# A new order of loads and of steps, and tiled matmuls for the first batch, in a kernel of windowed attention followed by two large products

## The chip, the cores and the metric

The kernel runs on one core of a Trainium2 chip. Time is the device time of one execution in microseconds (us), as the median of a kernel's runs. Each execution has a state: slow, when it is over 1.5% longer than the fastest of the same kernel, otherwise fast. The ratios below are the record's: fast runs of one kernel against fast runs of the kernel before in the same rounds on the same chip, with a 95% interval, so they are not quite the ratio of the medians beside them, which are of all runs. Where a ratio is turned into us, it is multiplied by 352, the median of the kernel before.

## The reference

```python
# q, k, v: 8 batches x 8 heads x 576 x 64;  w_in: 512 x 2048;  w_out: 2048 x 512
scores = scale * q @ k.T              # kept where 0 <= row - column < 64
attn   = softmax(scores) @ v
x = attn.transpose(0, 2, 1, 3).reshape(4608, 512)
h = x @ w_in
g = h - tanh(h)
out = g @ w_out
```

The 4608 rows of x are worked in nine chunks of 512. A batch is 576 rows, so a chunk needs one or two batches.

## The kernel before

A chunk takes 16 steps of the first product ("h", four matmuls of 512 columns into one bank of PSUM, the memory that TensorE writes its results to, then a tanh on ScalarE and a subtraction on VectorE that gives the bank back) and 16 steps of the second ("y", also four matmuls; four such steps fill a bank, which ScalarE then copies out). The order of steps alternates: one h of this chunk, one y of the chunk before.

```python
def hp_mm(c, m):                       # one h step
    hp = ps[:, m % 2, :]               # two banks in turn
    for ki in range(4):
        nc.tensor.matmul(hp, w_in_tile(ki, m), chunk_tile(c)[...], start=(ki == 0), stop=(ki == 3))
    th = sm_pool.tile([128, TOK], F32, tag="th", name="th")
    nc.scalar.activation(th, hp, ACT.Tanh)
    return hp, th

def g_sub(c, m, hp, th):
    nc.vector.tensor_tensor(gT[c][:, m, :], hp, th, ALU.subtract)

def yp_bank(c, s):
    return (0, 2)[s % 2] if c == NC - 1 else 2      # one bank for y, except in the last chunk
# ... (cut)
LAG = 16
for h in range(min(items), 2 * (16 * NC + LAG) + 2):
    n = h // 2
    # even h: hp_mm of step n;  odd h: yp_mm of step n - 16
    # then whatever of attention is listed for this step (items), then g_sub
```

Attention and loads are listed per step. The part ahead of the first step, the prologue, is a script. Of its letters, `V1`, `K1`, `Q1` are loads of the second batch, `w0` to `w2` pieces of w_in, `k05s` and the like the copies of V that give the keys of one window (vw from vb, nine to a batch; the last letter is the issuing engine: p GpSimd, s SyncE, a ScalarE; VectorE then copies what they brought from the upper 64 partitions of vw to the lower 64, which is called the shift), `P0` a second product of attention with its normalization:

```python
PLAN = {
    -1: """ ... k08s k00s b1p k03p n k02s F0a E0av R01 R02 q2p E1av k07p V1 k06a a3p k04p b2v K1 a2a
            R00 F1v k05s r3a E2aa F2a Q1 w0 R10 z0v ... P0 R11 E3aa R20 P1 ... w1 ... Q2 R32 P3 ...""",
    # ... (cut)
    12: "a8v R41 o2 o1 a9p d20p z1v",
    15: "R50 o3 R40 ... o0 d23p P5 k25s R60",        # o0 to o3: the pieces of w_out
```

The softmax here doesn't subtract the row's maximum and nothing guards it: scores larger than these inputs give would overflow.

## Time and profile before

| kernel before | |
|---|---|
| time | 351.54 us, median of 3 (351.35 to 354.38) |
| span of the profiled run | 351.4 us |
| TensorE busy (PE) | 315.1 us, 90% |
| VectorE, ScalarE | 199.0 and 192.8 us |
| first matmul of the first product | 38.2 us |
| first product of the second chunk | 70.7 us |

TensorE is the bound once the prologue is over. To read its stretches, compare the length with the busy time of PE. The second and third chunk (columns: stretch, length, busy us of PE, PEld, DVE, ACT, POOL, then clock, DMA share and GB/s; PE is TensorE's matmuls, PEld its weight loads, DVE VectorE, ACT ScalarE, POOL GpSimd, further on SP SyncE, and a q behind a name is that engine's instruction queue):

```profile
71.70:107.00 35.30, 33.72 (x247) 19.02 (x246) 23.91 (x38) 20.49 (x38) 14.61 (x19) 1.00 0.79 148
107.00:142.40 35.40, 35.04 (x263) 20.14 (x261) 24.56 (x40) 22.26 (x42) 17.32 (x22) 1.00 0.78 134
```

A chunk lasts some 35 us and TensorE works in all but 0.4 to 1.6 us of it. VectorE and ScalarE are busy for two thirds of that time, which says nothing about how soon a single bank comes back; this matters below.

### The profile page before, as it was taken

What the parts mean: (1) busy time and instruction counts of PE and PEld (TensorE: products, weight loads), DVE (VectorE), ACT (ScalarE), POOL (GpSimd) and SP (SyncE); (2) the same over time, 40 slices, a digit from 0 to 9 for tenths busy, and PEclk for the clock granted to TensorE, in tenths of its full rate; (3) what the DMA queues carried; (4) which work ended last, traced back from release to release, by engine and by line L of the source; (5) the groups of instructions that cost most, each with busy time, mean ns of one, the idle gap of its engine ahead of it and who ended that gap; (6) DMA issues with size and microseconds to landing.
All of it is one profiled execution on the core that took longest, in us unless ns stands there. A gap on an engine that the chain in (4) does not pass through costs nothing.

```text
span 351.4 us, 5740 instructions
## 1 busy us (share of the span) xinstructions
PE 315.1 (90%) x2173; PEld 179.0 (51%) x2173; DVE 199.0 (57%) x314; ACT 192.8 (55%) x347; POOL 112.0 (32%) x160
## 2 busy tenths in 40 slices
PE   0267788899899999999999999997999999999995
PEld 0256366555555555555555555553555444444442
DVE  1336786867676666666776766663656333344400
ACT  1467479765556665666566666652554444444411
POOL 7829543833338325422642264410000000000000
PEclk9988999999999999999999999998999999999999
DMA  8699999969777696958494895669711400010021
GB/s 175 126 164 190 175 189 173 183 133 180 161 148 112 127 137 146 139 126 156 102 160 105 164 169 123 130 147 206 189 46 38 121 32 30 31 60 30 30 89 62
DMA packets 54436, 43.98 MB, mean 125 GB/s; under 512 B 25144, under 2 KB 48248, under 8 KB 54024
## 3 DMA queue, kind: packets, MB, share of 16 engines
q0 software_dynamic: 20512, 18.22, 35.8%
q1 hardware_dynamic: 33128, 24.37, 27.0%
q10 hardware_dynamic: 768, 1.02, 1.0%
q8 instruction: 17, 0.28, 0.3%
q14 instruction: 11, 0.09, 0.1%
HBM read 36.70 MB, written 11.21 MB: 136 GB/s over the span
## 4 chain that ended last, share of the span: by engine, by line
PE 78%; DVE 7%; DMA 5%; ACT 5%; POOL 2%; issue 2%; SPq 0%; ACTq 0%; DVEq 0%; POOLq 0%
PE ps L324 34%; PE ps L304 32%; PE ps L261 5%; PE ps L247 4%; DVE xs L272 3%; PE ps L234 3%; DMA vw<-vb 3%; DMA vall<-in_v_dram 2%; DVE gT L314 2%; ACT th L308 1%; DVE qt L84 1%; ACT pt L251 1%; ACT qt L82 1%; DMA kt<-kd 1%; DVE pt L255 1%
## 5 line engine op out<-in xcount | busy, mean ns | idle before, releaser
L314 DVE TENSOR_TENSOR gT<-ps,th 128x512 bf16<-128x512 f32 x144 | 99.3, 691 | 94.9 <-ACT th L308 92.6
L304 PE MATMUL ps<-xT,wi 128*128 128x512 bf16 x576 | 147.7, 380 | 1.7 <-DVE gT L314 1.7
L324 PE MATMUL ps<-w_out_sb,gT 128*128 128x512 bf16 x576 | 146.1, 381 | 0.2 <-ACT ysb L329 0.2
L308 ACT ACTIVATE th<-ps 128x512 f32<-128x512 f32 x144 | 85.9, 597 | 79.8 <-PE ps L304 79.5
L304 PEld LDWEIGHTS <-wi 128*128 128x128 bf16 x576 | 61.4, 114 | 47.7 <-issue 3.6
L324 PEld LDWEIGHTS <-gT 128*128 128x128 bf16 x576 | 54.3, 98 | 55.9 <-issue 1.0
L251 ACT ACTIVATE pt<-ps 128x384 bf16<-128x384 f32 x96 | 46.9, 490 | 44.9 <-PE ps L247 38.3
L272 DVE TENSOR_TENSOR xs<-ps,rc 64x576 bf16<-64x576 f32 x64 | 48.3, 755 | 1.5
L84 POOL COPY vb<-vall 72x1024 bf16<-72x1024 bf16 x29 | 30.6, 1069 | 52.8 <-DMA vall<-in_v_dram 40.2
L247 PE MATMUL ps<-qt,kt 128*128 128x128 bf16 x288 | 36.4, 226 | 8.5 <-ACT pt L251 3.8
L261 PEld LDWEIGHTS <-pt 128*128 128x128 bf16 x288 | 22.7, 101 | 19.8 <-issue 3.6
L261 PE MATMUL ps<-vw,pt 128*128 128x130 bf16 x288 | 29.6, 226 | 3.4 <-DVE xs L272 1.1
L247 PEld LDWEIGHTS <-kt 128*128 128x128 bf16 x288 | 24.4, 102 | 12.1 <-DMA kt<-kd 2.1
L329 ACT ACTIVATE ysb<-ps 128x512 f32<-128x512 f32 x36 | 21.5, 597 | 16.0 <-PE ps L324 16.0
L84 DVE COPY qt<-ps 64x576 bf16<-64x576 bf16 x24 | 18.2, 759 | 18.1 <-ACT qt L82 18.1
L84 POOL COPY kb<-kall 96x768 bf16<-96x768 bf16 x26 | 21.7, 837 | 13.0 <-DMA kall<-in_k_dram 12.1
L84 POOL COPY qb<-qall 96x768 bf16<-96x768 bf16 x24 | 20.0, 832 | 16.8 <-DMA qall<-in_q_dram 16.8
L82 ACT ACTIVATE qt<-ps 64x576 bf16<-64x576 bf16 x32 | 20.3, 636 | 1.0 <-PE ps L234 0.6
L82 ACT ACTIVATE kt<-ps 128x576 bf16<-128x576 bf16 x25 | 16.2, 648 | 4.3 <-PE ps L234 4.0
L255 DVE TENSOR_TENSOR pt<-pt,ps 128x1152 bf16<-128x1152 bf16 x24 | 17.9, 745 | 0.0
L234 PE MATMUL ps<-ident,kb 96*128 96x96 bf16 x168 | 12.2, 210 | 2.7 <-ACT xT L82 0.9
L234 PEld LDWEIGHTS <-kb 96*128 96x128 bf16 x168 | 10.2, 100 | 7.4 <-issue 2.7
(52 smaller groups left out, 123.4 us busy)
## 6 DMA issues: line engine op xcount, KB each, us to landing
out_dram<-ysb SPq DMA_DIRECT2D x36, 256.0 KB
vall<-in_v_dram POOLq DMA_DIRECT2D x7, 576.0 KB, 10.0
kall<-in_k_dram POOLq DMA_DIRECT2D x7, 576.0 KB, 8.8
qall<-in_q_dram POOLq DMA_DIRECT2D x7, 576.0 KB, 8.8
vw<-vb SPq DMA_DIRECT2D x61, 65.0 KB
vw<-vw SPq DMA_DIRECT2D x6, 520.0 KB
w_out_sb<-in_moe_w_out_dram POOLq DMA_DIRECT2D x4, 512.0 KB, 8.4
qd<-qz SPq DMA_DIRECT2D x4, 288.0 KB
```

The source lines that it names most:

```text
L82: nc.scalar.activation(o, i, ACT.Copy)
L84: eng.tensor_copy(o, i)
L234: nc.tensor.transpose(tp[:, e, :], src[:, e, :], ident[:P, :P])
L247: nc.tensor.matmul(sp[:, i, :], kT[g % NR][:, 64 * j:64 * j + 128], qT[g % NR][:, :, 64 * j:64 * j + 64], start=True, stop=g >= 2 * NP)
L251: nc.scalar.activation(PT[g % NPT][:, 3 * grp:3 * grp + 3, :], sp, ACT.Exp, scale=scale)
L261: nc.tensor.matmul(ps[:, 5 + grp, 130 * i:130 * i + 130], PT[g % NPT][:, j, :], vw[b % 2][:, j, 2 * pr:2 * pr + 2, :], start=True, stop=True)
L272: nc.vector.tensor_tensor(xo[r, :, :, pr, :], ov[r, :, :, h, 0:D], rc[r].to_broadcast([64, 3, 3, 64]), ALU.mult)
L304: nc.tensor.matmul(hp, w_in_tile(ki, m), chunk_tile(c)[:, :, ki % 2, 64 * (ki // 2):64 * (ki // 2) + 64], start=(ki == 0), stop=(ki == 3))
L308: nc.scalar.activation(th, hp, ACT.Tanh)
L314: nc.vector.tensor_tensor(gT[c][:, m, :], hp, th, ALU.subtract)
L324: nc.tensor.matmul(yp, gT[c][:, m, s * 128:(s + 1) * 128], w_out_sb[:, m, :], start=(m == 0), stop=(m == M - 1))
L329: nc.scalar.activation(ysb, ps[:, yp_bank(c, s), :], ACT.Copy)
```

## The change

It means to shorten the prologue. The first batch's attention uses tiles of 64 rows or columns of the TensorE array, with VectorE's normalization in one instruction over all partitions. Both weights are loaded ahead of the second batch. The first chunk goes through both products alone, so that TensorE has work while the second batch arrives. Cut to its core:

```diff
+    def pair_of(banks):
+        a, b = banks
+        return ps[:, a:b + 1:b - a]
+    def tile_scores(g, grp, banks):   # ... 64-row tiles, one exponential over a pair of banks
+    def tile_pv(g, banks):            # ... 64-column tiles, one normalization over a pair of banks
 def hp_mm(c, m):
-        hp = ps[:, m % 2, :]
+        hp = ps[:, m % 3 if c < 2 else m % 2, :]
 def yp_bank(c, s):
-        return (0, 2)[s % 2] if c == NC - 1 else 2
+        return (2, 0)[s % 2] if c == NC - 1 or (c < 2 and s < 2) else 2
+    HS = [0, 32] + [30 * c for c in range(2, NC)]       # step at which each chunk's h begin
+    MOE = []
+    for c in range(NC):
+        ys = len(MOE) - M * c
+        y_left = M * c - ys
+        end = HS[c + 1] - HS[c] if c + 1 < NC else 2 * M
+        hs = [("h", c, m) for m in range(M)]
+        early = [("y",) + divmod(ys + i, M) for i in range(min(y_left, end - M))]
+        late = [("y",) + divmod(ys + len(early) + i, M) for i in range(end - M - len(early))]
+        # ... 16 h with the early y spread among them
+        MOE += mixed + late
+    # first batch: cast V, warm(9), tile_scores(0, 0, (0, 4)), tile_scores(0, 1, (1, 7)), warm(6),
+    # keys_v(0, ...), load_w_in(0), ... load_w_in(1), ... load_w_out(0..3)
+    for pr in range(NP):
+        at(3, load_v, 1, pr)
+    for g in range(4, 8):
+        at(4, load, g, "k", G)
+        at(4, load, g, "q", G)
+    for j in range(NJ):
+        at(22, keys_v, 1, j, Y if j < 5 else A)
+    # ... second batch's attention at steps 24 to 31, third batch's at 33 to 58
+    for j in range(NJ):
+        at(33 + j // 3, keys_v, 2, j, Y)
-    LAG = 16
-    for h in range(min(items), 2 * (16 * NC + LAG) + 2):   # h and y in alternation
+    for h, op in enumerate(MOE):
```

`warm(n)` issues n matmuls whose result is not used.

## The prediction

> **What bounds the kernel now.** I read the page's slices first, then a table of busy times in stretches, then the chain of work that ended last in order of time, then the timelines of GpSimd (it issues the loads) and of TensorE.
>
> The slices (each 8.8 us):
>
> ```profile
> PE   0267788899899999999999999997999999999995
> ...
> PEclk9988999999999999999999999998999999999999
> DMA  8699999969777696958494895669711400010021
> ```
>
> From the ninth slice TensorE is at 9 in nearly every slice, and the DMA row falls. In the first eight it is the other way round: the DMA is at 9, TensorE is not. The stretches make it exact (columns: stretch, its length, busy us of PE, PEld, DVE, ACT, POOL, then clock, DMA share, GB/s):
>
> ```profile
> 20.00:30.00 10.00, 6.63 (x68) 5.86 (x69) 4.53 (x8) 6.53 (x12) 3.90 (x4) 0.66 1.17 192
> ...
> 50.00:55.00 5.00, 3.42 (x61) 3.09 (x59) 3.91 (x7) 4.27 (x9) 2.72 (x4) 1.00 1.00 145
> ...
> 65.00:70.00 5.00, 4.13 (x29) 2.27 (x28) 3.81 (x8) 3.58 (x8) 4.63 (x7) 1.00 1.01 194
> 70.00:80.00 10.00, 10.00 (x64) 5.21 (x62) 5.87 (x10) 6.38 (x12) 4.36 (x5) 1.00 0.69 127
> 80.00:90.00 10.00, 10.00 (x81) 6.00 (x80) 7.59 (x12) 5.57 (x10) 2.61 (x4) 1.00 1.05 203
> ```
>
> Up to 70 us the DMA share is about 1; from 70 us TensorE is busy 10.00 of 10.00. So there are two stages: a prologue of some 70 us bound by transfers and by short dependent steps, and 280 us bound by TensorE alone. The chain shows what the prologue waits for:
>
> ```profile
> 2.93 6.30 DMA vall<-in_v_dram
> ...
> 16.57 9.21 DMA vw<-vb
> 25.86 0.71 DVE vw L167
> 26.61 0.61 PE ps L261 x4
> ...
> 33.67 0.77 DVE xs L272
> ...
> 40.81 1.04 PE ps L304 x4
> ```
>
> The keys' copy of V (vw from vb), issued at 16.57, lands only after 9.21 us, behind the second batch's V, whose load was issued at 14.96. Then four rounds of product, reciprocal and two half-height multiplications run one after the other, and the first matmul of the first product (L304) starts at 38.2. The GpSimd timeline shows the loads' order:
>
> ```profile
> 33.18 0.80 POOL L176 DMA_DIRECT2D wi<-in_moe_w_in_dram  x1
> ...
> 34.74 0.81 POOL L101 DMA_DIRECT2D qall<-in_q_dram  x1
> ...
> 37.85 0.76 POOL L176 DMA_DIRECT2D wi<-in_moe_w_in_dram  x1
> ...
> 48.74 0.97 POOL L151 DMA_DIRECT2D vall<-in_v_dram  x1
> 51.37 1.12 POOL L184 DMA_DIRECT2D w_out_sb<-in_moe_w_out_dram  x2
> ...
> 62.28 0.53 POOL L184 DMA_DIRECT2D w_out_sb<-in_moe_w_out_dram  x1
> ```
>
> The third batch's Q, K and V stand between the weights. The last piece of w_out took about 7 us and so landed at 69.3; the second product (L324) starts at 71.8, when 17 of the 144 steps of the first have been done in 34 us, for want of anything else to feed TensorE.
>
> **What the Trainium skill says.** "DMA: Bandwidth & Descriptors", Issuing engines are not separate DMA queues: DMAs started by any engine share the same 16 DMA engines and interleave. The trace agrees: the copy above took 9.2 us beside a load, others 3.9 us. So the order of issue decides what arrives first. "TensorE: Matmul & The Clock Gate", Back-to-back issue gap: N/2.4 + 2.5 ns, 216 ns for 512 columns; here four such matmuls take 0.86 us, so agreed. The same page, What's actually happening: the clock is halved when TensorE has idled and comes back after some 3.4 us of work; here 0.66 in 20 to 30 us. The added dummy matmuls aim at that. "TensorEngine Tiling (Array Packing)", PSUM Bottleneck: tiling speeds up TensorE but not the evacuation of PSUM. No run here shows tiles yet. I take it as the reason to count the tiles' gain on VectorE and ScalarE, not on TensorE.
>
> **The change, part by part.**
>
> First batch in tiles. Per head pair the multiplication is one over 128 partitions x 640 in place of two of 64 x 576 (755 ns each, so 1.51 us); by its columns one takes about 0.84 us. The exponentials are two (640 and 512 columns) in place of three of 384 (490 ns). Between 384 columns (490) and 512 (597) a column costs 0.84 ns, so 0.70 + 0.60 = 1.30 us against 1.47. Q is evacuated once on ScalarE (0.65) in place of ScalarE then VectorE (0.64 + 0.76). VectorE so saves about 1.4 us per pair in the round that is the chain: four rounds of some 1.1 us instead of 2.0. Tiled matmuls with 64 or 65 columns I put at the 43 ns of a 96-column transposition: 20 x 43 ns is 0.86 us per pair for the second product of attention, against 0.51 before. That is 0.35 us worse, hidden in the first batch, and 1.4 us in the second.
>
> Keys earlier. The casts of V move to ScalarE and VectorE right after its landing (8 to 9.5 us), so the nine copies are issued at about 11 to 14 us, with no second batch's V ahead of them, and land at 18 to 20 us instead of 25.9. Shift (1.4), four rounds (4.4), transpositions and their evacuation (1.5): the first product starts at about 27 us instead of 38.2.
>
> Weights ahead of the second batch. From the landings between 34.8 us (first w_in piece) and 62.5 (second w_out piece), 8.8 MB of float32 arrived in 27.7 us, 318 GB/s. Over the first 75 us, with copies and gaps, it is 20.2 MB, 278 GB/s. The first batch (3.5 MB) and all weights (8.4 MB) at 278 GB/s from 2.2 us on: 45 us. The first chunk's 16 steps of the first product run from 27 to 41 us, and its second product needs the last w_out piece after three more steps, 44 us: a stall of 1 to 2 us. The order of instructions shows a further tie: a GpSimd load waits for the one eight places earlier, so V of the second batch waits for w_in, and K for w_out; with the others still in flight this should not empty the queues.
>
> First chunk alone, then the second batch. After the first chunk all of its 32 steps are done. The second batch's data are complete at 2.2 + 15.5 MB / 278 GB/s = 58 us. After the last K: cast 0.83, transpositions and evacuation 1.2, then in TensorE's order three and a half steps (3.0), six score groups of 0.33 us (2.0), three tiled products (2.6), transpositions of x (1.0) and about 1 us of VectorE and ScalarE latency at the end: 11.6 us. The second chunk therefore starts at about 69.5 us.
>
> Added at the end of the prologue: x of the third batch is transposed on TensorE, 18 x 56 ns = 1.0 us. Chunks of 30 steps instead of 32 let the first product run ahead; TensorE's sum is unchanged.
>
> Sum. From the second chunk on there remain 256 steps of four matmuls of 512 columns, at 0.8632 us: 221.0. Attention: 20 head pairs with transpositions 0.52, scores 0.50, product 0.51, 30.6 in all; four pairs without transpositions 4.0; x 1.0. Together 256.6. Check on the kernel before: at 71.8 us 271 steps (233.9) and 32.3 us of attention remain, 266.2; its last matmul ends at 347.4, so 9.4 us went to waits (5.2 us named in TensorE's timeline, 1.9 of them for kt from kd at 240 us; the clock of 0.68 after that wait cost some 1.8 more). I keep 9.4, as the later batches' code is the same. From the last matmul to the end 4.0. So 69.5 + 256.6 + 9.4 + 4.0 = 339.5. Against 351.5: TensorE has done 15 more steps (12.9 us) at a time 2.3 us earlier, less about 3.3 us of third-batch attention that is not yet done or is added.
>
> **The rivals.** First: the second batch comes too late, and the wait moves from the weights to it. For it: the ring of eight, the V path (cast 4.2 us on GpSimd, copies, shift) that holds all of the TensorE order behind its first tiled product, and ScalarE's some 14 us of work in that part. Against: DMA is fed continuously. It would put the second chunk at 75 us: 345. Second: a pure stretch of first products needs 0.60 us of ScalarE and 0.69 of VectorE per 0.86 us of TensorE, so once the third batch's attention is mixed into the second chunk, VectorE and ScalarE can bound it. For it: VectorE's sum there is about 15 us against TensorE's 17.6, close with in-order engines. Against: three banks instead of two for the first product. It would cost 2 to 4 us: 342. Third: the new spacing also removes the late wait for kt from kd and its halved clock; that gives 3 to 4 us more: 336. Fourth: transfers alone set the prologue and nothing is gained; against it, 278 GB/s would then have to fall below 230, which only the first 20 us show.
>
> **Range and chances.** The start of the second chunk is uncertain by about 4 us, the waits by 3. I predict 339.0 us, with 333.5 to 345.0 holding it 8 times in 10. Faster by over 2% means below 344.5: 0.87. Within 2%: 0.11. Slower: 0.02.
>
> **What would show it.** In the changed kernel the copies to vw should land by 20 us; the first matmul of the first product should start at 25 to 29 us; the last w_out piece land near 45; the first product of the second chunk start at 67 to 72; TensorE be busy over 95% from there; and its last matmul lie 4 us before the end. The first product starting after 33 us would fell the step on tiles and keys; a gap over 3 us before the second chunk, named by vall, kall or vw, would mean the first rival; gaps named by ScalarE or VectorE in the second chunk, the second.

## The result, and the profile after

The changed kernel takes 397.67 us (median of four runs, 394.19 to 400.45, the slowest of them slow, so that the ratio rests on three) against 351.97 us for the kernel before in the same rounds: ratio 1.1221 (1.113 to 1.1311). It is slower by 43 us, where 12 us less were predicted. The profiled run was fast: span 392.5 us, clock 0.965.

The slices of the changed kernel, each 9.8 us:

```profile
PE   6668996689488878778887899799989999999995
...
PEclk9975999889879999999999999999999999999999
DMA  9999959374605774672776458785696031001012
```

TensorE starts earlier, as was meant. But from the seventh slice to the twenty-third it is mostly at 8 or below, where the kernel before stood at 9 in nearly all from its ninth slice on. The DMA row is no longer full either, so transfers are not what fills these slices. The stretches of the changed kernel's second-batch part and next three chunks:

```profile
51.30:87.30 36.00, 27.04 (x278) 16.93 (x282) 12.24 (x22) 13.31 (x28) 15.63 (x19) 0.91 0.71 122
87.30:135.20 47.90, 37.03 (x277) 21.55 (x282) 26.19 (x41) 25.11 (x48) 12.93 (x17) 0.93 0.49 86
135.20:178.00 42.80, 33.77 (x247) 19.47 (x250) 24.14 (x37) 22.48 (x43) 17.65 (x23) 1.00 0.66 119
178.00:218.00 40.00, 33.73 (x238) 19.05 (x240) 22.96 (x36) 21.51 (x40) 13.23 (x18) 1.00 0.60 106
```

Compare with the two lines of before: TensorE's work is 37.0 us in the second chunk and then 33.8 and 33.7, much as before, and the chunks are 5 to 13 us longer. Some records are missing (542 of 576 second-product matmuls are in the trace; 34 at 0.216 us are 7 us), so the idle time is overstated by up to that in all.

To follow this through all kernels I use one mark, the start of the first tanh of a chunk in the trace, and at the end the last copy of y. In us, with chunk 1 the first:

| kernel (profiled run) | 1 | 2 | 3 | 4 | 5 | 6 | 7 | 8 | 9 | last y |
|---|---|---|---|---|---|---|---|---|---|---|
| before | 39.4 | 71.9 | 108.2 | 143.3 | 178.6 | 212.4 | 249.1 | 279.2 | 306.8 | 347.5 |
| after | 36.8 | 88.2 | 136.2 | 178.8 | 218.9 | 255.6 | 291.2 | 321.2 | 347.1 | 388.6 |

The predicted sum can be set against this, line by line: the second chunk's first matmuls came at 87.3 us (one alone at 86.7) in place of 69.5 (17.8 us). From there to the last matmul, at 388.5, are 301.2 us; 256.6 us of work were counted, so 44.6 us lie beyond it, in place of 9.4 (35.2 us). They are not all waits: the trace has TensorE idle for 35.7 us there (overstated by up to the 7 us above), and the rest is work that took longer than counted, part of it at half clock (0.50 from 105.7 to 112.5 us). In the kernel before, the idle time from 71.8 us on is 5.2 us. The tail is 4.0 us, as predicted. 339.5 + 17.8 + 35.2 = 392.5 us, the span (the run's time, 394.19 us, is 1.7 us longer). So there are two things to explain: a late second chunk, and slow chunks after it.

### The profile page after: what moved, and what is told of

It reads as the page before. It is cut to its first block, busy times and chain, and to the rows that moved or that the text cites. A ratio compares the mean times of both kernels' runs of the same rounds, so it can differ in the third digit from the quotient of the medians.

```text
span 392.5 us, 5974 instructions
## 1 busy us (share of the span) xinstructions
PE 330.6 (84%) x2277; PEld 182.5 (47%) x2312; DVE 196.4 (50%) x316; ACT 186.6 (48%) x339; POOL 111.9 (29%) x159
## 4 chain that ended last, share of the span: by engine, by line
PE 61%; DVE 13%; DMA 13%; ACT 8%; issue 2%; SPq 1%; POOL 0%; ACTq 0%; DVEq 0%; POOLq 0%
PE ps L346 26%; PE ps L366 24%; DVE xs L313 5%; DMA vw<-vb 4%; DMA vw<-vw 4%; DVE gT L356 3%; PE ps L302 3%; DMA xT<-xs 3%; DVE qt L85 2%; PE ps L238 2%; PE ps L288 2%; DMA qall<-in_q_dram 2%; ACT th L350 1%; ACT pt L266 1%; ACT ysb L371 1%
## 5 line engine op out<-in xcount | busy, mean ns | idle before, releaser
L366 PE MATMUL ps<-w_out_sb,gT 128*128 128x512 bf16 x542 | 138.0, 382 | 14.2 <-ACT ysb L371 9.7
L346 PEld LDWEIGHTS <-wi 128*128 128x128 bf16 x576 | 62.3, 114 | 61.3 <-issue 15.4
L292 ACT ACTIVATE pt<-ps 128x384 bf16<-128x384 f32 x84 | 40.7, 488 | 45.5 <-PE ps L288 35.9
L313 DVE TENSOR_TENSOR xs<-ps,rc 64x576 bf16<-64x576 f32 x48 | 36.2, 755 | 1.1
L371 ACT ACTIVATE ysb<-ps 128x512 f32<-128x512 f32 x36 | 21.4, 595 | 27.1 <-PE ps L366 22.8
L85 POOL COPY kb<-kall 96x768 bf16<-96x768 bf16 x29 | 23.9, 827 | 35.2 <-PE ps L238 19.2
L288 PE MATMUL ps<-qt,kt 128*128 128x128 bf16 x252 | 29.7, 223 | 3.2 <-ACT pt L292 2.0
L302 PE MATMUL ps<-vw,pt 128*128 128x130 bf16 x216 | 23.4, 223 | 6.5 <-DMA vw<-vw 6.5
L302 PEld LDWEIGHTS <-pt 128*128 128x128 bf16 x216 | 17.8, 99 | 21.3 <-issue 4.7
L288 PEld LDWEIGHTS <-kt 128*128 128x128 bf16 x252 | 20.9, 100 | 12.3 <-issue 3.8
L85 POOL COPY qb<-qall 96x768 bf16<-96x768 bf16 x20 | 16.6, 828 | 10.4 <-DMA qall<-in_q_dram 6.0
L83 ACT ACTIVATE qt<-ps 64x576 bf16<-64x576 bf16 x24 | 15.3, 636 | 3.2 <-PE ps L238 3.1
```

The lines of the kernel that those rows point to most:

```text
L83: nc.scalar.activation(o, i, ACT.Copy)
L85: eng.tensor_copy(o, i)
L288: nc.tensor.matmul(sp[:, i, :], kT[g % NR][:, 64 * j:64 * j + 128], qT[g % NR][:, :, 64 * j:64 * j + 64], start=True, stop=g >= 2 * NP)
L292: nc.scalar.activation(PT[g % NPT][:, 3 * grp:3 * grp + 3, :], sp, ACT.Exp, scale=scale)
L302: nc.tensor.matmul(ps[:, 5 + grp, 130 * i:130 * i + 130], PT[g % NPT][:, j, :], vw[b % 2][:, j, 2 * pr:2 * pr + 2, :], start=True, stop=True)
L313: nc.vector.tensor_tensor(xo[r, :, :, pr, :], ov[r, :, :, h, 0:D], rc[r].to_broadcast([64, 3, 3, 64]), ALU.mult)
```

## The experiments

Two theories were set against each other. A: the order of steps. An h with no y behind it asks for its bank again too soon, and a run of y in one bank waits for each copy. B: the order of loads and copies. The second and third batch come late, and TensorE, which works in the order of the program, stops at them.

### The order of steps

**Runs in the kernel before.** Only the order of steps is changed there, in chunks three to seven (counted from one, as everywhere below outside the quoted texts; the texts count the first chunk as 0, or not at all): 16 h with 6 y among them, then 10 y.

```diff
+    EARLY = 6
+    for c in range(2, 7):
+        # 16 h, the first EARLY y spread among them, then the other y
+        ORDER[32 * c:32 * c + 32] = mixed + ys[EARLY:]
```

> The kernel before with one thing of the change alone: in chunks 2 to 6 the 32 steps are no longer first product, second product in turn, but 16 first products with 6 second ones among them, then 10 second ones in a run (the changed kernel has 4 to 12 among, then 10 to 2). Loads, tiles and the attention's slots stay. Theory A, the order of the steps costs the time (in a run of first products the tanh and the subtraction do not hide, in a run of second ones the single bank waits for its evacuation): each of the five chunks grows by 3 to 6 us, total 366 to 380. Theory B, the order is harmless and the later chunks are slow because data come late: within 1.5% of before, under 357.

Measured: 381.33 us, ratio 1.0748 (1.071 to 1.0785), output correct. Chunks three to seven take 45, 39, 41, 39 and 35 us where before has 35, 35, 34, 37 and 30. So the order alone costs 26 us in a kernel whose loads, copies and tiles are untouched. That is just above theory A's range, and theory B's "no change" is refuted.

The timeline of TensorE in this run shows one such wait (start, length, what, and in brackets the idle time before it and what ended it):

```profile
196.80 1.03 PE L304 MATMUL ps<-xT,wi 128*128 128x512 bf16 x4
...
197.92 1.03 PE L304 MATMUL ps<-xT,wi 128*128 128x512 bf16 x4
...
200.56 1.02 PE L304 MATMUL ps<-xT,wi 128*128 128x512 bf16 x4 [1.44 <-DVE gT L314]
```

These are three h steps one after the other with two banks. The third needs the first one's bank, which comes back after 200.56 - 196.80 = 3.76 us: four matmuls, the tanh behind whatever ScalarE has in hand, the subtraction behind whatever VectorE has. In the kernel before, the same bank is asked for later:

```profile
144.30 1.03 PE L304 MATMUL ps<-xT,wi 128*128 128x512 bf16 x4
...
148.60 1.03 PE L304 MATMUL ps<-xT,wi 128*128 128x512 bf16 x4
```

Here one h lies between the two (at 146.36), and two y: 4.30 us. The y steps in between are what hides the round trip.

**Twelve among.** The same with 12 of the 16 y among the h, so that 4 h of a chunk and not 10 are bare (have no y behind them).

```diff
-    EARLY = 6
+    EARLY = 12
```

> As the run with runs in the kernel before, but 12 of the 16 second-product steps stand among the 16 first-product steps of chunks two to six, and 4 in a run after them, where that run had 6 and 10. Theory A (the cost is first-product steps with no second-product step behind them): 4 bare steps instead of 10, so 0.4 of its 27 us: 360 to 367 us, chunks two to six at 36 to 38 us. Rival (what costs is the attention standing at other places, whatever the length of the runs): 373 to 385 us.

Measured: 363.39 us, ratio 1.0308 (1.0248 to 1.0369), as theory A expected. The waits of TensorE over the whole run, for the bank of the first product (on gT) and of the second (on ysb), as total us, times, longest. The kernel before (its ysb wait is 0.2 us, in the page's groups):

```profile
PE ps L304 <- DVE gT L314: 1.7, 3, 0.6
```

Twelve among:

```profile
PE ps L304 <- DVE gT L314: 6.1, 13, 0.9
PE ps L324 <- ACT ysb L329: 5.0, 5, 1.1
```

Six among:

```profile
PE ps L304 <- DVE gT L314: 18.6, 23, 1.7
...
PE ps L324 <- ACT ysb L329: 8.8, 10, 1.1
```

In all three kernels 1.7 us of the gT wait fall in the first chunk. With 20 bare h steps in five chunks the two waits are then 9.4 us there, with 50 they are 25.6 us: 0.47 and 0.51 us for each. The times rise by 11 and 26 us, 0.54 and 0.53 us a bare step. (In both traces 31 of the 576 second-product matmuls are missing, so the waits are overstated somewhat.) The dose, the named waits and the total time agree.

**A second bank for y.** In the changed kernel, some runs of y get a second bank.

```diff
     def yp_bank(c, s):
+        if (c, s) in ((2, 0), (3, 0), (4, 0), (5, 0)):
+            return 0
+        if (c, s) == (2, 1):
+            return 1
```

> The changed kernel with the second product's result alternating between two banks where its steps run one after another in chunks 2 to 5. Theory A: the waits of second-product steps for the evacuation (9.7 us in all in the changed kernel) fall to about 4, the time by 4 to 6 us. Rival B: TensorE then waits at the next data instead, time within 1%.

Measured: 397.91 us, ratio 1.1278 (1.1215 to 1.134), so no gain. The wait for ysb, 9.7 us in the changed kernel, is gone from the top of the list, and in its place h waits 6.4 us for the transposed x of the next batch (three times, up to 3.9 us), while the wait for gT stays at 8.4 us. A wait that is taken off a run of y is spent at the next tie. The rival's number is met; that the whole order was late there is argued, not shown. The y half of theory A was not worth mending alone.

**Alternation in the changed kernel.** The changed kernel with the order of before from the second chunk on; attention is moved to the steps that correspond.

```diff
-    HS = [0, 32] + [30 * c for c in range(2, NC)]
+    HS = [0] + [32 * c - 16 for c in range(1, NC)]
+    MOE = [("h", 0, m) for m in range(M)]
+    for c in range(1, NC):
+        for m in range(M):
+            MOE += [("h", c, m), ("y", c - 1, m)]
+    # second batch's attention all at step 15
```

> The changed kernel, its tiles, loads, banks and dummy matmuls kept, but the step order of the kernel before: the first chunk's 16 first-product steps alone, then from the second chunk on one first-product step and one second-product step of the chunk before in turn; the attention's slots are moved with it. The second chunk then starts with none of the first chunk's second product done, so TensorE idles through the second batch: its start at 78 to 86 us. Theory A, the order of steps is what makes the later chunks slow: from there each chunk takes 33.7 to 36 us as in the kernel before, so 256.6 + 13.8 + 9 + 4 after a start near 82: 365, range 358 to 371, though 16 more steps are left at that point than in the changed kernel. Theory B, later data are late: chunks stay at 37 to 48 us, total 385 or more.

Measured: 384.06 us, ratio 1.0877 (1.0826 to 1.0928), but the output was wrong. The second batch's attention at step 15 wrote into bank 0 before the subtraction of that same step, which came after it in the program, had read it. The program's order itself was wrong. The time lies between what A and B expected, and is read no further. Mended, with the subtraction of that step ahead of the attention:

> The changed kernel with the order of steps of the kernel before, as in the alternate run, with its fault mended: the subtraction of the first chunk's last step now stands ahead of the second batch's attention, which wrote over its bank. Theory A (the order of steps): correct output, 380 to 388 us, chunks four and later back at 33 to 36 us each, so some 12 us less than the changed kernel. Rival (the speed came from the wrong output or from the fault): 392 to 400 us.

Measured: 383.24 us, correct, ratio 1.0861 (1.0803 to 1.0918). That is 0.036 below the changed kernel, or 13 us, give or take some 4, as theory A expected; the rival's 392 to 400 is refuted. The profiled run, with a clock of 0.554, is not read; the ratio is of its three fast runs. In the changed kernel the two named waits are

```profile
PE ps L366 <- ACT ysb L371: 9.7, 10, 1.3
PE ps L346 <- DVE gT L356: 8.4, 15, 1.6
```

18.1 us in all, 17.1 of them in chunks three to eight, which have 42 bare steps (0.41 us each). The second chunk, whose h have three banks, has none of the two. So the order, with the slots of attention, casts and loads and the banks of y that moved with it, is worth 13 us of the 43; that other waits take up the rest of the 17 is likely, but not shown, and whether the later chunks went back to 33 to 36 us this run can't say.

### The first batch

**Neighbouring banks.** The scores of one pair of heads use banks (0, 4) and (1, 7). `pair_of` addresses such a pair as one strided slice, and the program's tracking of dependences seems to take all that lies between as touched. The changed kernel's timeline shows what this does to the scores' second group, in banks 1 and 7, which waits for the exponential of banks 0 and 4:

```profile
10.80 0.59 PE L257 MATMUL ps<-hide,ident 128*128 128x256 bf16 x2 [2.02 <-ACT pt L266]
```

```diff
-    tile_scores(0, 0, (0, 4))
-    tile_scores(0, 1, (1, 7))
+    tile_scores(0, 0, (0, 1))
+    tile_scores(0, 1, (4, 5))
     # and so for every pair of banks
```

> The changed kernel with the pairs of PSUM banks that a tile's evacuation reads made neighbours (0 and 1, 4 and 5, 6 and 7) instead of 0 and 4, 1 and 7, 0 and 7. The built program then lacks the waits of the second score group, of the dummy matmuls and of second-product steps for an evacuation of banks that they do not share. Theory C, these waits hold the prologue: the first matmul of the first product at 29 to 31 us instead of 34.6, the second chunk at 78 to 83 instead of 87.3, total 5 to 9 us less. Rival, transfers and casts set the prologue: first product not before 33, total within 1%.

Measured: 389.51 us, ratio 1.102 (1.0993 to 1.1047), 7 us less than the changed kernel. The mark of the first chunk falls from 36.8 to 34.3 us and that of the second from 88.2 to 81.0: most of the gain is in the second batch, whose banks were tied in the same way. The first matmul came at 32.0 us, a little after the 29 to 31 expected; the rival's "not before 33" is refuted. With the ties gone, another wait ends last in the first batch. TensorE has the scores of the first two pairs of heads done at 16.4 us and then waits for the shift (5.43 us until 22.55), and the shift for a copy of V, of which the chain of this run says:

```profile
14.10 9.42 DMA vw<-vb
```

SyncE issued it at 13.09 us, behind the first piece of w_in (12.62).

**No idle matmuls.** `warm(6)` and `warm(2)` are taken out.

```diff
-    warm(6)
-    warm(2)
```

> The changed kernel without the six and two dummy matmuls between the first batch's head pairs (the nine at the start stay). They run at the halved clock (six took 2.72 us) ahead of the second pair's transpositions. If they stand in the way: first product 2 to 3 us earlier, total 2 to 3 us less. If they keep the clock up, more matmuls run at half clock and the first product starts within 1 us of 34.6 or later.

Measured: 396.44 us, ratio 1.1266 (1.1205 to 1.1328), the same as the changed kernel. The first chunk is 1.4 us earlier (35.4), the second no earlier in effect (88.0). The six stood on the chain for 2.72 us at half clock. They did bring the full clock, from 16.9 to 23.8 us, where without them it is 0.50 from 9.4 to 36.7; yet the chunk comes earlier without them, and the gain is lost by the second. Neither expectation fits quite.

**The first batch without tiles.** `scores` and `pv` with `norm` in place of `tile_scores` and `tile_pv`.

```diff
-    tile_scores(0, 0, (0, 4))
-    tile_scores(0, 1, (1, 7))
+    scores(0, 0, 4)
+    scores(0, 1, 0)
+    scores(0, 2, 1)
     # and so for the four pairs of heads; pv and norm in place of tile_pv
```

> The changed kernel with the first batch's attention as in the kernel before (128 x 128 and 128 x 130 matmuls, three exponentials, two half-height multiplications), all else kept. The prediction put the tiles' gain at about 0.9 us per head pair: first product 3 to 5 us later, total 3 to 5 us more. Theory C's rival, that the tiles' bank pairs cost what they save: first product within 1.5 us of 34.6, total within 1%.

Measured: 404.4 us (395.77 to 411.51), ratio 1.1283 (1.1191 to 1.1376), correct. Two of its four runs were slow, so the ratio rests on two. Its profiled run was slow too, so its 40.1 us for the first chunk (3.3 later than with tiles) is only an indication. The ratio's interval covers that of the changed kernel: whatever the tiles give, it does not reach the end clearly.

### Loads and copies

**Keys early.** In the changed kernel the copies that give the second batch its keys are listed at step 22, four of them issued by ScalarE. Its DMA queues, ScalarE's first, then SyncE's:

```profile
55.01 4.79 ACTq L162 DMA_DIRECT2D vw<-vb  x4
```

```profile
56.11 7.81 SPq L162 DMA_DIRECT2D vw<-vb  x5
64.08 23.98 SPq L373 DMA_DIRECT2D out_dram<-ysb  x3
88.24 6.49 SPq L162 DMA_DIRECT2D vw<-vb  x9
```

V of the second batch had been cast by 50.8 us, but step 22 came at 55. The third batch's copies stand behind three outputs in SyncE's queue, which works in order: they go out at 88.24. The experiment lists both earlier, all on SyncE:

```diff
-        at(22, keys_v, 1, j, Y if j < 5 else A)
+        at(16, keys_v, 1, j, Y)
-        at(33 + j // 3, keys_v, 2, j, Y)
+        at(30, keys_v, 2, j, Y)
```

> The changed kernel with the second batch's copies of V for the keys given right after the first chunk's first product and all by SyncE (not by SyncE and ScalarE after six steps of the second product), and the third batch's at slot 30 instead of 33 to 35. Theory D, those copies hold the second chunk: first tiled product of the second batch at 60 to 63 us instead of 69, second chunk at 80 to 83 instead of 87.3, total 4 to 7 us less. Rival: the second batch's ScalarE and VectorE work is the bound there: second chunk within 2 us of 87, total within 1%.

Measured: 387.98 us, ratio 1.0969 (1.0926 to 1.1013), 9 us less than the changed kernel. The second chunk did not come earlier (mark 90.1, against 88.2): the copies went out from 50.5 us on, but the shift that follows them on VectorE still began only at 68.0. It came straight after VectorE's evacuation of the second batch's last transposed q (67.22, 0.76 us): it stands behind two of these in VectorE's order, so the order of steps held it, and not the copies. The second batch's first product came at 69.5 us (69.1 in the changed kernel), so neither that nor the second chunk came as theory D expected, though the total fell by more than it said. The gain is in the chunk after it: third mark 131.0 in place of 136.2, and the third batch's copies went out at 71.4. In the changed kernel TensorE waits there for the third batch's shifted V,

```profile
105.74 1.03 PE L302 MATMUL ps<-vw,pt 128*128 128x130 bf16 x8 [4.60 <-DMA vw<-vw]
```

and its clock is 0.50 from there to 112.5 us. With the keys early both are gone.

**Weights first in the kernel before.** One part of the change alone: all of w_in ahead of the second batch, whose keys are then turned inside the first chunk.

```diff
-   ... E1av k07p V1 k06a a3p k04p b2v K1 a2a
+   ... E1av k07p w0 w1 w2 V1 k06a a3p k04p b2v K1 a2a
     # w0, w1, w2 taken from where they stood
-        0: "b8p",
+        6: "b4v b7v b5p F4a b6p b9p E4vv b8p",     # taken from the script ahead of step 0
```

> The kernel before with only the order of loads of the change: the whole of the first weight ahead of the second batch, and the second batch's keys turned inside the first chunk instead of ahead of it. Theory B (weights first moves the first product little and the second batch's attention late): first product 0 to 4 us earlier than the 39 us of before, second chunk not earlier than 71.9, 349 to 358 us. Rival (the prediction's own reading, that the first product is bound by the loads ahead of it and everything after moves with it): first product 5 us or more earlier and 343 to 347 us.

Measured: 366.27 us, ratio 1.0409 (1.0353 to 1.0465), slower by 14 us; both theories missed. The first chunk's mark is at 49.8 us, ten later than before. The chain of this run, and what GpSimd had issued just ahead of it:

```profile
18.40 17.94 DMA vw<-vb
```

```profile
14.53 2.27 POOL L176 DMA_DIRECT2D wi<-in_moe_w_in_dram  x3
```

The last of the first batch's key copies, 65 KB, is issued behind all of w_in and the second batch's V and takes 17.94 us to land; in the kernel before it took 9.21 us behind that V alone. The changed kernel pays some 3 us of this. It issues its nine copies between 10.2 and 14.5 us, w_in from 12.88 on. The four that GpSimd issued, all ahead of w_in, landed in 3.8 to 4.3 us each; but the last two of SyncE's five went out behind w_in's first piece, and VectorE's second shift waited for a copy until 23.24 us. This run's 14 us are therefore not the changed kernel's loss; it shows which neighbour a small copy must not have.

**Keys first, in the kernel before.** The opposite, as it was meant: the nine copies ahead of the second batch's V. This is the step of the prediction on the keys, tried by itself.

```diff
-   k08s k00s b1p k03p n k02s ... E1av k07p V1 k06a a3p k04p b2v
+   k08s k00s b1p k03p k07p k04p n k02s ... E1av k06s V1 a3p b2v
```

> The kernel before with one part of the change: all nine copies of the first batch's keys are issued ahead of the second batch's V load. If the prologue's chain carries through: first product at 34 to 36 us (39.4 before), 346 to 349 us. Rival (the second chunk waits for the last piece of the second weight, landed at 69.3 us, whatever the first product does): first product earlier as well, second chunk still at 71 to 72 us, 350.5 to 353 us.

Measured: 354.41 us, ratio 1.0051 (0.9999 to 1.0104): the same. The first chunk did not come earlier: mark 39.2 against 39.4. The edit does less than was meant. Seven of the nine copies go out ahead of the second batch's V (issued at 15.14 us), but one, `k05s`, stays behind `V1` in the script, and the last two of SyncE's were issued at 15.47 and 16.84 us. VectorE's second shift waits for a copy about as long as before (there 3.66 us until 25.86):

```profile
26.01 0.70 DVE L167 COPY vw<-vw 64x2080 bf16<-64x2080 bf16 x1 [3.06 <-DMA vw<-vb]
```

The chain also holds Q of a later pair of heads until 20.40 us, whose load now stands behind the copies in GpSimd's order. The time missed both expectations, the rival's narrowly; its second chunk at 71 to 72 us is met (71.7). What keys wholly ahead of V are worth in the kernel before is not shown.

**And w_out together.** The edit of the last run, with the four pieces of w_out issued at step 12.

```diff
-        12: "a8v R41 o2 o1 a9p d20p z1v",
+        12: "a8v R41 o2 o1 o3 o0 a9p d20p z1v",
     # o3 and o0 taken out of step 15
```

> As the keys-first run, and the four pieces of the second weight are issued together at one step instead of the last one three steps later, behind GpSimd's casts. If the rival of the keys-first run holds: second chunk at 67 to 70 us and 347 to 350 us, below the keys-first run by 2 to 4 us. If the prologue's chain alone counted: the same as the keys-first run within 1 us.

Measured: 353.11 us, ratio 1.0018 (0.9978 to 1.0058): the same, and the second chunk's mark stayed at 71.8; the copies still held the second shift, until 25.44 us. The last piece of w_out was issued at 53.9 us instead of 62.3, but the four now took up to 15.0 us to land, so the last was there by 69.0 at the latest, against some 69.3 before. The run did not bring w_out clearly forward. Whether w_out holds the second chunk of the kernel before, its own trace can say: its second product begins at 71.77 us with no idle time of TensorE ahead of it, 2.5 us after the last piece had landed, so w_out did not hold it there.

### Together

**All of it.** The changed kernel with alternation, neighbouring banks, the second batch's loads ahead of w_out, and its keys' copies early on SyncE. The first form shared the fault of the alternating run (output wrong):

```diff
     # alternation and neighbouring banks as above
-    for i in range(4):
-        load_w_out(i)                  # ahead of the second batch
+    for i in range(4):
+        at(6, load_w_out, i)           # behind the second batch
-        at(14, keys_v, 1, j, Y if j < 5 else A)
+        at(8, keys_v, 1, j, Y)
```

> As e5, and also: second batch's Q, K and V loaded ahead of w_out (w_in still ahead of both), its copies of V for the keys given by SyncE during the first chunk, and the neighbouring banks of e2. If the waits found so far add up, the first product starts near 31, the second chunk at 58 to 64 us, total 341 to 350, which is under the kernel before. Rival: the second batch's work on ScalarE and VectorE, with nothing for TensorE beside it, holds the second chunk until 70 or later: total 352 or more.

Measured: 374.59 us, ratio 1.062 (1.0573 to 1.0667). Mended as above:

> The run with the order of before, the second batch's loads ahead of the second weight, the keys' copies issued early by SyncE and neighbouring banks, with the same fault mended. Theory A: correct output, 370 to 378 us, as the faulty one's 374.6; chunks four and later 33 to 36 us, chunks one and two still 45 to 48 us, as their length is the second and third batches' attention. Rival (the fault made the time): 385 us or more.

Measured: 373.96 us, correct, ratio 1.0599 (1.0534 to 1.0663), 22 us less than the changed kernel. From the fourth chunk on it keeps the pace of before (35, 34, 34, 31 and 28 us). The second and third still take 45.4 and 45.7. In the third, TensorE has one wait for the fourth batch's V, and SyncE's queue shows why:

```profile
123.74 0.38 PE L302 MATMUL ps<-vw,pt 128*128 128x130 bf16 x2 [7.06 <-DMA vw<-vw]
```

```profile
87.40 16.27 SPq L373 DMA_DIRECT2D out_dram<-ysb  x2
103.78 6.93 SPq L162 DMA_DIRECT2D vw<-vb  x9
117.88 0.52 SPq L170 DMA_DIRECT2D vw<-vw  x1
```

**The fourth batch's V earlier.**

```diff
-    at(31, load_v_all, 3)
+    at(24, load_v_all, 3)
     # its casts 5 steps, its copies and its shift 5 steps earlier
```

> The mended combination with the fourth batch's V loaded 7 steps and its copies issued 5 steps earlier, ahead of outputs in SyncE's queue. If the wait of 7 us for these copies is what the third chunk lost: 364 to 368 us and the third chunk at 38 to 40 us instead of 45.7. Rival (another wait takes its place, or the attention of two batches in too few steps is the cost): 371 to 376 us.

Measured: 363.7 us, correct, ratio 1.037 (1.0301 to 1.044; the record calls its verdict unclear): 8 us less than the version before it, and the third chunk lasts 36.3 us. Marks of the last two versions:

| kernel (profiled run) | 1 | 2 | 3 | 4 | 5 | 6 | 7 | 8 | 9 | last y |
|---|---|---|---|---|---|---|---|---|---|---|
| all of it, mended | 34.3 | 70.3 | 115.7 | 161.4 | 196.6 | 230.4 | 264.6 | 295.1 | 322.7 | 364.2 |
| fourth V earlier | 34.7 | 71.3 | 116.6 | 152.9 | 188.2 | 222.0 | 255.6 | 286.1 | 313.7 | 355.2 |

The last version's prologue is 4.7 us shorter than that of the kernel before, its first chunk 4.1 us longer, its second 9.0 us longer. It is still slower than the kernel before by its ratio; no version tried is faster than that.

## Why the prediction was wrong

It was wrong in direction: 339.0 us predicted with 0.87 for faster, 397.67 measured.

- **"The first product starts at about 27 us."** It started at 34.6 (first matmul). The term that failed is "four rounds of some 1.1 us" behind copies that land by 20 us: the scores were taken for hidden, the copies for early. The chain of the changed kernel shows the scores' exponentials instead, the second of each pair of heads at

```profile
18.61 0.61 ACT pt L266
...
22.92 0.61 ACT pt L266
...
28.01 0.61 ACT pt L266
...
28.66 0.78 PE ps L276 x20
```

  4.3 and 5.1 us apart, each with transpositions, evacuation, mask, two groups of scores and two exponentials in a row; the products (L276) wait for them. Neighbouring banks took 2.6 us off this (first matmul at 32.0). What is left can be read in that run. Its shift ended at 24.3 us, 2.9 later than the prediction's 21.4 (copies by 20, shift 1.4), for the copies behind w_in. From there to the first product it took 7.6 us in place of 5.9 (four rounds 4.4, transpositions 1.5), 1.7 more. These three, 2.6, 2.9 and 1.7 us, are nearly all of the 7.6 that the start was late, by one profile each.

  A rival within these terms is the clock, which no run separates. In the changed kernel it was half until after the first product had begun:

```profile
23.80:37.40 13.60, 10.16 (x137) 6.55 (x134) 5.54 (x12) 4.40 (x8) 2.74 (x5) 0.50 1.08 212
```

  From 23.6 to 34.8 us TensorE's pieces of the chain add up to 7.4 us, so up to half of that, 3.7 us, may be due to it (an estimate from the chain). The added dummy matmuls did not hold the clock up to here.

- **"w_out lands at 44", "the second batch's data are complete at 58 us".** Both came earlier: the last piece of w_out landed at 39.8 us, the last load of the second batch at 48.4, and its V was cast by 50.8. So the first rival, late loads, is not it either.

- **"The second chunk starts at about 69.5 us."** Its first matmul came at 87.3. The 11.6 us for the second batch's attention were summed as if each engine could start when the data are there. They were tied to step 22 for the copies and to steps 24 to 31 for the rest. The first transposition came at 59.1 us, over ten after the data had landed, behind y steps that stood ahead of it in the order; from there to 87.3 it took 28.2 us in place of 11.6. TensorE was busy for 18.9 of the last 27.4 us, at 0.88 of the clock (0.50 from 75.0 to 81.8). Freed bank ties gave 7 us in all, 4.7 of them here by the marks. Issuing the copies 4.5 us earlier gave nothing, as the shift stood behind two evacuations of q in VectorE's order. No run accounts for the rest of these 28.2 us.

- **"I keep 9.4, as the later batches' code is the same", "TensorE's sum is unchanged".** This is the step that cost most: 44.6 us lay beyond the counted work in place of 9.4. The code of attention is the same, but the order of steps that hides its latencies and those of h is not. The second rival, pure stretches of the first product, named the place at "2 to 4 us" and looked at busy sums (VectorE 15 of 17.6 us). What counts is the round trip of one of two banks, 3.8 us as measured, against the time until the order asks for it again, and in runs of y the copy of the one bank. The change spends all y of the first chunk at once, so that chunks three to six have only 4 to 10 y among their 16 h. Shown: 0.53 us a bare step in the kernel before, at two doses; 13 us in the changed kernel, with what moved along. The third batch's copies behind outputs in SyncE's queue are another 9 us, half-clocked work behind the wait for them included: they were moved in one run with the second batch's, whose part gave nothing that the marks show.

- **Third rival** (the late wait for kt from kd disappears, 336 us): that wait was 1.9 us in the kernel before, and whether it vanished plays no part beside 43 us. **Fourth rival** (transfers alone set the prologue): the second batch had landed over ten us before its first transposition, so no.

Of the prediction's readings, the sizes of single operations held (multiplication 0.83 us for 0.84, exponentials 0.71 and 0.61 for 0.70 and 0.60). The second w_out piece landed at 63.6 us in the kernel before, not 62.5, which makes the 318 GB/s some 306 (worked out anew).

What stays open: 13 us of the last version against the kernel before, by the ratio. Its profiled run was its fastest, and its last y comes 7.7 us later by the marks: 4.7 less in the prologue, 4.1 more in the first chunk, 9.0 in the second and 1.2 in the third, 1.9 less after that. TensorE also has more to do in its second chunk (busy for 38.3 us of 45.3, against 34.7 of 36.3 before), as the whole third batch's attention falls there. In its first chunk the clock is 0.50 from 52.0 to 65.7 us with TensorE busy for 11.8 of them, which may cost up to 5.9 us (an estimate, half of the busy time): more than what is lost there, and tested by no run. The gains of the single runs are also not additive: 13, 7 and 9 us alone, 22 us in the combination, which moves a load as well.

## What to carry to other kernels

An order of steps is itself a buffer: before you group steps of one kind, set the measured round trip of its bank (matmul, ScalarE, VectorE, with what stands ahead of each) against the time until the bank is asked for again, and don't take over the waits of the old order. Give every term of a predicted chain its predecessor in the new program, on every engine and queue; a wait that is removed is worth only the distance to the next one. Small copies on which much depends go out ahead of bulk loads, and not behind outputs in a queue that works in order.

## What the Trainium skill lacked or had wrong

- "Perfetto Trace Analysis", Matmuls, says that independent matmul groups should rotate through different banks. It gives no way to tell how many an order of steps needs: here two banks are enough in alternation with y (asked for again after 4.30 us) and not enough without (round trip 3.76 us; 0.53 us lost per bare step).
- "DMA: Bandwidth & Descriptors", Issuing engines are not separate DMA queues, is right that transfers share the engines, and 17.94 us for a copy of 65 KB behind all of w_in, against 3.8 to 4.3 us for those that the changed kernel issued from GpSimd ahead of w_in, shows how far this goes. It calls the time to start a DMA usually small beside the DMA; four issues of such copies on ScalarE's queue took 4.79 us in all (0.62 to 1.87 us each), about as long as one of those early copies needed to land.
- "TensorEngine Tiling (Array Packing)", Instruction Overhead, gives some 60 cycles as the floor of a matmul. The prediction overlooked it and put 43 ns; 20 tiled matmuls of 65 columns took 0.44 us at full clock in the second batch, 22 ns each, so the page was the better source. In the first batch the same 20 took 0.78 us, at a clock of 0.50.
- No page that I found says that a strided slice over two banks that are not neighbours can tie the banks between them in the program's order: 7 us here, the tie itself being inferred from the wait that went.
